# Moving the ring of streamed weight sums from 64 to 128 modulo 256 bytes in each partition

## The chip, the cores and the metric

The kernel runs on one core of a Trainium2 chip. The metric is device time in microseconds (us) of one launch, lower being better. Times come from plain runs, and from one profiled execution whose trace has a span from its first to its last instruction.

## The reference, cut to what matters

```python
# attention: batch 4, 8 heads, 768 rows, head dimension 64, fp32
k_sum = k.reshape(B, H, nb, 32, D).max(axis=3)          # one summary key per 32 rows
v_sum = v.reshape(B, H, nb, 32, D).mean(axis=3)
scores_l = where(|i - j| < 16, scale * q @ k.T, -1e9)   # local window
scores_s = scale * q @ k_sum.T + log(32)                # 24 summaries
a = softmax(concat([scores_l, scores_s]))
x = (a @ concat([v, v_sum]))  as 3072 rows of 512
# feed-forward: 512 -> 2048 -> 512
r = maximum(x @ w_in, 0)
out = (s * r * r + b) @ w_out
```

## The kernel before, in words

The 3072 rows are worked through in 12 chunks of 256, c = 0 to 11. For each chunk the kernel computes the windowed attention, then the first product (`hidden`, L512, into the PSUM tile `ph`), then square, scale and offset, then the second product into the output. The second product is `project` (L557) in chunks 0 to 3 and `project_seven` (L677) in chunks 4 to 11. The work of one chunk's attention is laid between the previous chunks' products. One long string, `ORDER`, written out by hand, sets in which order all of it is issued; no scheduler reorders it. In `ORDER`, `H7.12` is `hidden(7, 12)`, `p7.6.2` is `project_seven(7, 6, 2)` and `j7.6.0` is `load_combo(7, 6, 0)`.

All large products split each fp32 factor into an upper part and a remainder of the type fp32r, and add three products (remainder times upper, upper times remainder, upper times upper). In `hidden`, weights `wl` and `wh` are loaded into TensorE as the stationary operand (LDWEIGHTS, 128 columns), and the attention result `xh` or `xl`, 256 columns, is streamed through as the moving operand.

`project_seven` takes the feed-forward width in 8 pieces q of two 128-row blocks. It is a two by two block product with seven instead of eight multiplications. So it has seven products of three matmuls, 21 matmuls for each q and 64 such groups of 21 in all (8 chunks, 8 pieces). Here the activations `gs` are the stationary operand and 256 columns of weights the moving one. For the products 0, 1, 3 and 5 the moving operand is a piece of the resident weights `wh` or `wl`. For the products 2, 4 and 6 it is a sum of weight blocks, which is computed once, kept in HBM as `combos`, and streamed back for every chunk into the ring. So in a group the matmuls stand as six with resident weights, three with the ring, three resident, three ring, three resident, three ring.

The ring is one tile, `arena.tile([P, RING])`, of 3136 floats in each partition. Six slices of 512 floats lie in it: for q even or odd, three parts n, each with 256 floats of upper and 256 of remainder. `load_combo` (L617) fills one slice by one DMA of 256 KB, issued from SyncE's queue: 2048 bytes to each of 128 partitions. It waits until the matmuls that read the slice two pieces earlier are done. In the last chunk the last two pieces (q = 6 and 7) don't use the ring but tiles named `late`, since their loads are issued ahead.

What matters for an address is where the program, as built, puts each tile in a partition. These places are the same before and after the change, save for the slices within the ring.

| operand | role | start in the partition, modulo 256 bytes | modulo 512 |
|---|---|---|---|
| `wh`, `wl` | stationary in L512, moving in L677 | 0 | 256 |
| `xh`, `xl` | moving in L512 | 192 | 448 |
| `gs` | stationary in L677 | 192 | 192 |
| ring slices | moving in L677 | 64 | 320 |
| `late` for q = 6 and for q = 7, n = 2 | moving in L677 | 64 | 320 |
| `late` for q = 7, n = 0 and 1 | moving in L677 | 32 | 32 |

The ring's tile itself starts at byte 135424, which is 0 modulo 256. The same bytes serve earlier as `spare`, work space that starts at the tile's beginning and isn't touched by the change.

Of the kernel before, what the change touches and what calls it, by code (L numbers as in the profile page):

```python
# [45 lines left out]
def windowed_attention_then_relu2_ffn(ctx, tc, qk, vwin, kt, vt, kq, vrow, wp, out):  # L46
# [553 lines left out]
    def ring_part(c, q, n):  # L600
        if "ring" not in held:
            held["ring"] = arena.tile([P, RING], F32R, name="ring", tag="ring")
        if c == NC - 1 and q > 5:
            if q == 7 and n < 2:
                if "late" not in held:
                    held["late"] = p3.tile([P, 2 * UNIT], F32R, name="late", tag="qk", bufs=2)
                return held["late"][:, 512 * n : 512 * (n + 1)]
            if ("late", q, n) not in held:
                held["late", q, n] = p3.tile([P, 512], F32R, name="late", tag="vw", bufs=4)
            return held["late", q, n]  # L610
        k = 16 + 512 * (3 * (q % 2) + n)
        return held["ring"][:, k : k + 512]

    STREAMED = (T2, T3, T4)
# [1 line left out]
    def load_combo(c, q, n):  # L616
        nc.sync.dma_start(ring_part(c, q, n).bitcast(F32), combos[q, :, STREAMED[n]].rearrange("p h d -> p (h d)"))  # L617
# [44 lines left out]
    def project_seven(c, q, n):  # L662
        gh, gl = halves[c, q]
        if (q, n) == (0, 0):
            acc["m"] = ps_v.tile([P, DM], F32, name="acc", tag="pav")
            acc["x"], acc["y"] = (ps_po.tile([P, DM], F32, name="acc", tag="po") for _ in range(2))
            acc["z"] = ps_t.tile([P, DM], F32, name="acc", tag="pt")
        a, part, odd, lo, bank, side = PRODUCTS[n]
        if part is None:
            wh, wl = (w[2 * q + odd][:, lo : lo + 256] for w in (w_h, w_l))  # L670
        else:
            both = ring_part(c, q, part)
            wh, wl = both[:, :256], both[:, 256:]
        k = slice(a * P, (a + 1) * P)
        to = acc[bank][:, 256 * side : 256 * (side + 1)]
        for m, (g, w) in enumerate(((gl, wh), (gh, wl), (gh, wh))):
            nc.tensor.matmul(  # L677
                to, g[:, k], w, start=(q == 0 and side == 0 and m == 0),
                stop=(q == NF // 2 - 1 and m == 2 and side == (bank != "m")),
            )  # L680
# [301 lines left out]
```

## Time and profile before

| | |
|---|---|
| median of three plain runs | 595.0 us (593.6, 595.0 and 1473.68) |
| the profiled execution's own time | 593.89 us |
| its span | 592.2 us |
| TensorE matmuls busy | 579.7 us, 98% of the span |
| TensorE weight loads busy | 551.2 us, 93% |
| VectorE, ScalarE, GpSimd busy | 429.7, 352.3, 313.6 us |
| loads into the ring | 186 DMAs of 256 KB |

In the profile, PE is TensorE's matmuls and PEld its weight loads; a row names line, engine, operation, output and inputs, shapes and a count. The durations given for one matmul include its way through the array, and successive matmuls overlap. So the pace of TensorE is read from the distance between the starts of successive rows, not from the durations. Time 0 of all rows is the start of the span.

### The profile page before, as it was taken

The page shows a single profiled execution, that of the slowest core. Times are in us where ns is not written, and L with a number is a line of the kernel's source. Part 1 is how long each engine was busy: PE and PEld are TensorE (multiplying, and loading weights), DVE is VectorE, ACT ScalarE, POOL GpSimd, SP SyncE. Part 2 cuts the span into 40 slices and gives each one's busy share as a digit, 9 for nine tenths or more (in the row PEclk, how much of TensorE's full clock was granted, in tenths as well). Part 3 has the DMA queues.
Part 4 walks back from the last instruction along what each step waited for, and adds up shares of the span by engine and source line. Part 5 has one row for each costly group of instructions (what it writes and reads, how often), then busy time and mean ns, then how long its engine had stood idle before and what let it go on. Part 6 is the DMA issues. An engine that isn't in the chain of part 4 may idle for free.

```text
span 592.2 us, 15380 instructions
## 1 busy us (share of the span) xinstructions
PE 579.7 (98%) x5816; PEld 551.2 (93%) x5816; DVE 429.7 (73%) x1025; ACT 352.3 (59%) x808; POOL 313.6 (53%) x499
## 2 busy tenths in 40 slices
PE   7999999999999999999999999999999999999996
PEld 6788888989899899999999999999999999999996
DVE  6999977889697497699689699696687687322323
ACT  5999899367587683744654654653563564423432
POOL 4330012353665485357856756766747655636653
PEclk9999999999999999999999999999999999999999
DMA  8999964267656977876867977667566665574540
GB/s 337 401 390 412 360 232 157 85 214 228 210 168 216 306 251 244 285 228 226 265 235 239 274 222 230 230 200 232 189 196 223 203 198 182 178 223 153 170 143 35
DMA packets 69881, 135.73 MB, mean 229 GB/s; under 512 B 7792, under 2 KB 18032, under 8 KB 69808
## 3 DMA queue, kind: packets, MB, share of 16 engines
q1 hardware_dynamic: 69808, 134.77, 68.7%
q8 instruction: 45, 0.74, 0.5%
q14 instruction: 28, 0.23, 0.1%
HBM read 115.72 MB, written 18.87 MB: 227 GB/s over the span
## 4 chain that ended last, share of the span: by engine, by line
PE 80%; DMA 9%; DVE 5%; ACT 3%; issue 1%; POOL 1%; SPq 0%; DVEq 0%; POOLq 0%; ACTq 0%
PE ph L512 38%; PE acc L677 25%; PE po L557 10%; DMA wraw<-in_wp_dram 6%; PE pav L444 3%; PE ps L312 3%; DMA parked<-wf 1%; ACT pr L354 1%; DVE wf L135 1%; DMA kq<-in_kq_dram 1%; DVE spare L335 1%; DVE wf L134 1%; POOL g L583 0%; ACT wraw L125 0%; DVE wl L150 0%
## 5 line engine op out<-in xcount | busy, mean ns | idle before, releaser
L598 DVE TENSOR_TENSOR gs<-g,gs 128x896 fp32r<-128x896 f32 x64 | 71.5, 1118 | 82.7 <-ACT gs L594 82.0
L570 ACT ACTIVATE g<-ph 128x512 f32<-128x512 f32 x64 | 38.3, 598 | 153.1 <-PE ph L512 148.2
L393 DVE STREAM_TRANSPOSE pT<-qk 32x256 f32<-32x256 f32 x288 | 125.6, 436 | 4.8
L677 PE MATMUL acc<-wh,gs 128*128 128x256 f32 x512 | 121.4, 280 | 0.2 <-DVE gs L598 0.2
L512 PE MATMUL ph<-xh,wl 128*128 128x256 f32 x760 | 118.9, 278 | 1.2 <-ACT r L520 1.0
L512 PE MATMUL ph<-xh,wh 128*128 128x256 f32 x760 | 117.4, 276 | 0.0
L512 PE MATMUL ph<-xl,wh 128*128 128x256 f32 x760 | 117.4, 276 | 0.0
L578 POOL TENSOR_SCALAR g<-g,sb_col 128x512 f32<-128x512 f32 x64 | 54.8, 856 | 114.0 <-ACT g L574 105.7
L512 PEld LDWEIGHTS ph<-xh,wl 128*128 128x128 f32 x760 | 103.0, 188 | 5.4 <-ACT r L520 1.2
L512 PEld LDWEIGHTS ph<-xl,wh 128*128 128x128 f32 x760 | 100.7, 188 | 0.0
L512 PEld LDWEIGHTS ph<-xh,wh 128*128 128x128 f32 x760 | 100.5, 188 | 0.0
L677 PE MATMUL acc<-ring,gs 128*128 128x256 f32 x558 | 95.9, 280 | 0.0
L677 PEld LDWEIGHTS acc<-wh,gs 128*128 128x128 f32 x512 | 91.3, 188 | 1.5 <-issue 0.8
L677 PEld LDWEIGHTS acc<-ring,gs 128*128 128x128 f32 x558 | 78.8, 188 | 0.0
L557 PE MATMUL po<-wh,gs 128*128 128x512 f32 x224 | 76.7, 394 | 0.5 <-DVE gs L544 0.5
L583 POOL TENSOR_TENSOR g<-g 128x256 f32<-128x256 f32 x64 | 72.0, 1125 | 4.8
L677 PE MATMUL acc<-wl,gs 128*128 128x256 f32 x256 | 71.3, 278 | 0.0
L594 ACT CAST gs<-g 128x896 fp32r<-128x896 f32 x64 | 59.9, 935 | 16.4 <-PE acc L677 12.1
L354 ACT ACTIVATE qk<-qk,mn 128x120 f32<-128x120 f32 x144 | 55.0, 384 | 6.8 <-DVE mn L335 5.5
L274 POOL COPY vw<-vsum 24x256 f32<-24x256 f32 x88 | 44.0, 536 | 20.4 <-DMA vw<-in_vwin_dram 10.6
L557 PEld LDWEIGHTS po<-wh,gs 128*128 128x128 f32 x224 | 42.1, 188 | 9.1 <-DVE gs L544 0.7
L557 PE MATMUL po<-wl,gs 128*128 128x512 f32 x128 | 50.2, 392 | 0.0
(133 smaller groups left out, 901.2 us busy)
## 6 DMA issues: line engine op xcount, KB each, us to landing
ring<-combos SPq DMA_DIRECT2D x186, 256.0 KB
wraw<-in_wp_dram SPq DMA_DIRECT2D x32, 512.0 KB
qk<-in_qk_dram SPq DMA_DIRECT2D x44, 369.0 KB
vw<-in_vwin_dram SPq DMA_DIRECT2D x48, 256.0 KB
combos<-spare SPq DMA_DIRECT2D x16, 512.0 KB
out_dram<-o SPq DMA_DIRECT2D x24, 256.0 KB
kraw<-in_kt_dram SPq DMA_DIRECT2D x12, 384.0 KB
spare<-parked SPq DMA_DIRECT2D x8, 512.0 KB
```

Source lines behind the costliest of these rows:

```text
L274: nc.gpsimd.tensor_copy(vw_t[c, p][WIN:KR, e], vsum[bi][WIN : WIN + NB, 2 * p + e, :].unsqueeze(1).to_broadcast([NB, NSUB, D]),)
L312: nc.tensor.matmul(o, qi, kw[r, i, :], start=True, stop=True)
L354: nc.scalar.activation(pr, pr, AF.Exp, bias=mn_of[c, p][:, n : n + 1], scale=-1.0, accum_out=sums_of(c, p)[:, n : n + 1])
L393: nc.vector.transpose(to[BLOCK * k : BLOCK * (k + 1), :, rows], src)
L512: nc.tensor.matmul(ph, w[:, kc * P : (kc + 1) * P], x[:, kc], start=(n == 0), stop=(n == len(terms) - 1))
L557: nc.tensor.matmul(po[c, t], a[:, t * P : (t + 1) * P], w[:, 512:], start=(f == 0 and n == 0), stop=(f == NF - 1 and n == len(terms) - 1),)
L570: nc.scalar.activation(gg[c, q][:, : 2 * T], ph_of.pop((c, q)), AF.Relu)
L578: nc.gpsimd.tensor_scalar(g, g, s_col, b_col, ALU.mult, ALU.add)
L583: nc.gpsimd.tensor_tensor(g[:, 4:6], g[:, 0:1].to_broadcast([P, 2, P]), g[:, 1:3], ALU.subtract)
L594: nc.scalar.copy(halves[c, q][0], gg[c, q][:, P:])
L598: nc.vector.tensor_tensor(gl, gg.pop((c, q))[:, P:], gh.bitcast(F32), ALU.subtract)
L677: nc.tensor.matmul(to, g[:, k], w, start=(q == 0 and side == 0 and m == 0), stop=(q == NF // 2 - 1 and m == 2 and side == (bank != "m")),)
```

## The change

```diff
         if c == NC - 1 and q > 5:
...
             return held["late", q, n]
-        k = 16 + 512 * (3 * (q % 2) + n)
+        k = 32 + 512 * (3 * (q % 2) + n)
         return held["ring"][:, k : k + 512]
```

Every slice of the ring starts 32 floats past the tile's beginning instead of 16, and so at 128 modulo 256 bytes (384 modulo 512) instead of 64 (320). The tile has room for that: the last slice ends at float 3104 of 3136. The change touches the addresses of 186 DMAs (where they write) and of 558 matmuls (from where they read the moving operand). The instructions, their order on each engine, their waits and the places of all other tiles stay as they are, the `late` tiles' too.

## The prediction

> **What bounds the kernel now.** First the page's busy shares and its chain, then the costliest groups.
>
> ```profile
> PE 579.7 (98%) x5816; PEld 551.2 (93%) x5816; DVE 429.7 (73%) x1025; ACT 352.3 (59%) x808; POOL 313.6 (53%) x499
> PE 80%; DMA 9%; DVE 5%; ACT 3%; issue 1%; POOL 1%; SPq 0%; DVEq 0%; POOLq 0%; ACTq 0%
> L677 PE MATMUL acc<-wh,gs 128*128 128x256 f32 x512 | 121.4, 280 | 0.2 <-DVE gs L598 0.2
> L512 PE MATMUL ph<-xh,wl 128*128 128x256 f32 x760 | 118.9, 278 | 1.2 <-ACT r L520 1.0
> L677 PE MATMUL acc<-ring,gs 128*128 128x256 f32 x558 | 95.9, 280 | 0.0
> ```
>
> TensorE is the bound, and 80% of the chain that ended last. The last column matters most here: before the 558 matmuls that read the ring TensorE idled 0.0 us, so no load into the ring was ever late enough to hold it. The change can therefore act in two ways: on the pace at which TensorE reads the ring, directly on the bound; or on the loads, if they grew by more than their slack.
>
> The clock takes no part, since the stretches of time show it fully granted where the ring is used (the first of these rows stands for the others up to 592 us, all at 1.00).
>
> ```profile
> 240.00:300.00 60.00, 60.00 (x709) 59.42 (x705) 49.06 (x133) 35.53 (x101) 38.11 (x67) 1.00 0.80 254
> ```
>
> **The pace of TensorE.** This is a piece of its timeline: one group of 21 (403.17 to 405.62), the 24 matmuls of the first product behind it, and the next group's first row. The columns are the start in us, the length of the merged row, and what it is.
>
> ```profile
> 403.17 0.28 PE L677 MATMUL acc<-wh,gs 128*128 128x256 f32 x1
> ...
> 403.86 0.51 PE L677 MATMUL acc<-ring,gs 128*128 128x256 f32 x3
> 404.20 0.28 PE L677 MATMUL acc<-wh,gs 128*128 128x256 f32 x1
> 404.32 0.28 PE L677 MATMUL acc<-wl,gs 128*128 128x256 f32 x1
> ...
> 404.56 0.52 PE L677 MATMUL acc<-ring,gs 128*128 128x256 f32 x3
> 404.91 0.28 PE L677 MATMUL acc<-wh,gs 128*128 128x256 f32 x1
> ...
> 405.26 0.52 PE L677 MATMUL acc<-ring,gs 128*128 128x256 f32 x3
> 405.62 0.62 PE L512 MATMUL ph<-xh,wl 128*128 128x256 f32 x4
> 406.08 0.62 PE L512 MATMUL ph<-xl,wh 128*128 128x256 f32 x4
> ...
> 408.35 0.28 PE L677 MATMUL acc<-wh,gs 128*128 128x256 f32 x1
> ```
>
> From start to start, every matmul here having 256 columns:
> - first product, settled: 406.08 to 408.35, 20 matmuls in 2.27 us, 113.5 ns each;
> - the six resident ones before the first ring product: 403.17 to 403.86, 0.69 us, 115 ns each;
> - from the end of the first ring product to the end of the group: 404.20 to 405.62, 12 matmuls in 1.42 us, 118.3 ns each.
>
> So TensorE has two paces, about 113.5 and 118 ns, and in this group it changes from the fast to the slow one at the first ring product. Within the slow stretch the ring costs no more than the resident weights: three ring matmuls take 0.35 us (404.56 to 404.91), three resident ones 0.36 us (404.20 to 404.56). The first four matmuls of the next product still take 0.46 us (405.62 to 406.08, 115 ns each), and then the fast pace is back.
>
> The slow pace does not need the ring, though. A chunk's first two groups come right after the attention's small matmuls, and are slow from their second matmul on, before any ring product:
>
> ```profile
> 425.32 0.39 PE L677 MATMUL acc<-wh,gs 128*128 128x256 f32 x1
> 425.55 0.28 PE L677 MATMUL acc<-wl,gs 128*128 128x256 f32 x1
> ...
> 426.14 0.52 PE L677 MATMUL acc<-ring,gs 128*128 128x256 f32 x3
> ...
> 430.38 0.62 PE L512 MATMUL ph<-xh,wl 128*128 128x256 f32 x4
> ```
>
> Five resident matmuls from 425.55 to 426.14 take 118 ns each, and all 41 from 425.55 to 430.38 take 4.83 us, 117.8 ns each. [...]
>
> **The change part by part.** Nothing is added, removed or reordered; two terms remain.
>
> *Reads, 558 matmuls.* At 64 modulo 256 they cost 280 ns of duration, as the resident ones at 0 do (rows above), and at the slow pace the same 117 to 118 ns. The matmuls of the first product read their moving operand at 192 and run at 113.5 ns. The last chunk's tiles named late, partly at 32, are close:
>
> ```profile
> L677 PE MATMUL acc<-late,gs x18: 278/282/287, 582.5 to 587.1; 128*128 128x256 f32 x18
> ```
>
> So none of 0, 32, 64 and 192 shows a price of its own beyond 2 ns of duration, and 128 was not seen. I take 0 for it. The bounds: the best case is that at 128 the first ring product no longer brings the slow pace. From 403.86 to 406.08, 19 matmuls take 2.22 us, and at 113.5 ns they would take 2.16 us: 0.063 us for a group. The chain shows how many groups are like that one up to 574 us, where TensorE stops being the bound (its last row of the first product is at 571.41): 44 single groups, of which the first and last rows stand here, and the pair at 556.14, whose 4.92 us shows that it too starts fast.
>
> ```profile
> 251.46 2.44 PE acc L677 x21
> ...
> 425.39 5.15 PE acc L677 x42
> ...
> 556.14 4.92 PE acc L677 x42
> ...
> 568.96 2.44 PE acc L677 x21
> 571.41 2.74 PE ph L512 x24
> ```
>
> 45 x 0.063 = 2.8 us. If ring products at 128 even led back to the fast pace, as the first product does, the seven pairs like that at 425.39 would gain too, each at most 4.83 - 41 x 0.1135 = 0.18 us, together 1.2 us, and the second group of the pair at 556.14 some 0.1 us. So the reads save at most 4.1 us. The worst case is priced under the rivals.
>
> *Writes, 186 loads.* Each moves 256 KB whichever way it lies. What hides them is the time between issue and use:
>
> ```profile
> 399.23 7.29 SPq L617 DMA_DIRECT2D ring<-combos  x6
> ...
> 409.03 0.51 PE L677 MATMUL acc<-ring,gs 128*128 128x256 f32 x3
> ```
>
> The first of the six at 399.23 is the part j7.7.0, which was waiting for the ring product of piece 5 to free the slice; it is first read at 409.03, 9.8 us later. The core moved 254 GB/s in the busiest stretch quoted, at which 256 KB are 1.0 us of transfer. A load could take several times as long before TensorE saw it. Cost: 0. Behind the waiting SyncE instruction stand other loads, but what it waits for is TensorE, whose order stays.
>
> [...]
>
> Sum: 593.89 us for the profiled execution, whose span is 592.2 us with 1.7 us around it, plus 0, makes **593.9 us**. The median of the plain runs, 595.0, lies 1.1 us higher and their lowest, 593.6, 0.3 us lower, which is the scatter I allow.
>
> **The rivals.**
>
> *The first ring product stops breaking the pace* (faster, within 2%). For it: the pace changes just where the first operand at 64 is read, and nothing else in the group is new there but a wait for a landed load and another slice of `gs`. The distance between moving and stationary operand modulo 512 is 192 in the first product, which restores the fast pace (448 - 256); it is 64 with resident weights (256 - 192), 128 with the ring, and would be 192 for the ring after the change. Against it: ring and resident matmuls run alike in the slow stretch, and that stretch arises without the ring too. It gives 593.9 - 2.8 = 591.1 us, or 589.8 us if the slow pairs are healed as well.
>
> [...]
>
> *Ring matmuls clash with weight loads at 128* (slower). [...] The largest step that the rows show is 404.20 to 404.32, 0.12 us against the settled 0.1135, so 6.5 ns: 558 x 6.5 ns = 3.6 us, and 597.5 us. It decides as soon as a ring matmul costs more than the 118 ns of the slow pace. For it: 128 was never seen, and TensorE has no idle time to hide it. Against it: four other places without such a cost. To be slower by 2% (11.9 us), it would have to be 21 ns for each ring matmul, three times the largest step seen.
>
> *The loads become late*: only if one took over 9.8 us in place of some 1 to 3. No row speaks for it, and I leave it 1 in 100. That the change fails to do what it says can be left out, as the ring's tile starts at 0 modulo 256.
>
> **How the numbers follow.** No change: 0.44, 593.9 us, with the scatter 593.5 to 595. The pace kept or restored: 0.33, 589.8 to 591.1 us. A clash in the ring's reads: 0.21, up to 597.5 us, and 0.01 of it beyond 2%. Late loads: 0.01. The remaining 0.01 is for a gain beyond 2%, for which no mechanism is in sight: all ring matmuls together are far from 21 ns above the fast pace. The range from 589.5 to 597.5 us takes in the bounds of both unknowns. About 2%, 11.9 us, is what a measurement of this kernel can tell from no change; every priced case lies within that, so faster 0.01, same 0.97, slower 0.02.
>
> **What the profile after would show.** If I am right, the timeline again shows 113.5 ns in the first product, 115 ns up to the first ring product and 117 to 118 ns behind it, groups of 2.44 us and pairs of 5.15 us in the chain. If the first rival holds, groups of 21 take about 2.39 us and ring matmuls start every 0.113 us. If the second holds, three ring matmuls take more than 0.36 us while resident ones stay. Idle time before the ring's matmuls, now 0.0, would mean late loads. What would make me wrong beyond the range is a cost of 128 in TensorE's reads that no other operand here has.

## The result, and the profile after

The changed kernel takes 600.84 us (median of 6 runs, 600.05 to 601.47) against 594.35 us for the kernel before (median of its runs on the same chip). The ratio is 1.0111, 95% interval 1.0088 to 1.0135: slower by about 6.5 us. One of the six launches before, of 1473.68 us, is far above all the others: the median hardly feels it, and the ratio leaves it out. The forecast was 593.9 us, and 600.84 lies above the range's upper end of 597.5.

The page of the kernel after, with the rows that answer to those of before:

```profile
PE 586.5 (98%) x5816; PEld 558.1 (93%) x5816; DVE 429.6 (72%) x1025; ACT 352.2 (59%) x808; POOL 311.7 (52%) x499
L677 PE MATMUL acc<-wh,gs 128*128 128x256 f32 x512 | 122.9, 283 | 0.2 <-DVE gs L598 0.2
L512 PE MATMUL ph<-xh,wl 128*128 128x256 f32 x760 | 120.8, 281 | 0.3 <-DVE wl L150 0.2
L512 PE MATMUL ph<-xl,wh 128*128 128x256 f32 x760 | 119.6, 280 | 0.0
L512 PE MATMUL ph<-xh,wh 128*128 128x256 f32 x760 | 119.6, 280 | 0.0
L677 PE MATMUL acc<-ring,gs 128*128 128x256 f32 x558 | 95.5, 280 | 0.0
```

TensorE is busy 6.8 us longer (586.5 after 579.7), which is the whole loss. But the 558 matmuls whose addresses changed are no dearer: 95.5 us in place of 95.9, and still no idle time before them. The first product, whose addresses nobody touched, is what costs more: 120.8 us in place of 118.9 in the first of its three groups, and 119.6 in place of 117.4 in each of the others.

The busy times by stretches place it. First before, then after; the columns are the stretch, its length, the busy time and count of PE, PEld, VectorE, ScalarE and GpSimd, then the granted clock (1.00 is full speed), the busy share of the DMA engines and GB/s. Each stretch ends shortly after the last first product.

```profile
244.00:575.00 331.00, 331.00 (x3389) 329.04 (x3388) 226.57 (x531) 166.11 (x388) 206.42 (x315) 1.00 0.68 215
```

```profile
244.00:581.00 337.00, 337.00 (x3379) 335.01 (x3378) 226.28 (x527) 165.35 (x387) 203.12 (x312) 1.00 0.66 210
```

From 244 us on, where the ring is in use, TensorE needs 6 us more for nearly the same number of matmuls, without a gap and at the full clock in both.

The chain of waits shows in which pieces. Two rows of the first product from the kernel before, whose groups of 21 took 2.44 us:

```profile
405.78 2.73 PE ph L512 x24
...
416.13 5.45 PE ph L512 x48
```

And after:

```profile
400.96 2.47 PE acc L677 x21
403.43 2.83 PE ph L512 x24
406.26 2.47 PE acc L677 x21
...
419.33 5.65 PE ph L512 x48
```

A group of 21 takes 2.47 us where it took 2.44. The 24 matmuls of the first product between two groups take 2.83 us where they took 2.73, and the double ones at a chunk's end 5.65 where they took 5.45. From the first group to the last first product either chain has 44 single groups, 45 single first products and 7 double ones: 44 x 0.03 + 45 x 0.10 + 7 x 0.20 = 7.2 us by these rounded rows, against 6.6 us that the span grew (592.2 to 598.8). Of the difference 0.4 us is found ahead of the first group, which starts at 243.07 us after and at 243.51 before; the rest is rounding.

A piece of the timeline of the kernel after, one group and the first product behind it:

```profile
406.09 0.28 PE L677 MATMUL acc<-wh,gs 128*128 128x256 f32 x1
...
406.80 0.52 PE L677 MATMUL acc<-ring,gs 128*128 128x256 f32 x3
407.15 0.28 PE L677 MATMUL acc<-wh,gs 128*128 128x256 f32 x1
...
408.21 0.51 PE L677 MATMUL acc<-ring,gs 128*128 128x256 f32 x3
408.57 0.63 PE L512 MATMUL ph<-xh,wl 128*128 128x256 f32 x4
409.04 0.63 PE L512 MATMUL ph<-xl,wh 128*128 128x256 f32 x4
...
411.39 0.28 PE L677 MATMUL acc<-wh,gs 128*128 128x256 f32 x1
```

Everything now runs at the slow pace. The six resident matmuls from 406.09 to 406.80 take 118 ns each (115 before), the three of the ring 0.35 us, and the first product from 408.57 to 411.39 takes 2.82 us, 117.5 ns each. Before, it was back at the fast pace of 113.5 ns after four matmuls. Now it never gets there, and hands the slow pace on to the next group.

### The profile page after: what moved, and what is told of

The parts are those of the page before. It is cut to its first block, busy times and chain, and to the rows that moved or that the text cites. A ratio compares the mean times of both kernels' runs of the same rounds, so it can differ in the third digit from the quotient of the medians.

```text
span 598.8 us, 15380 instructions
## 1 busy us (share of the span) xinstructions
PE 586.5 (98%) x5816; PEld 558.1 (93%) x5816; DVE 429.6 (72%) x1025; ACT 352.2 (59%) x808; POOL 311.7 (52%) x499
## 4 chain that ended last, share of the span: by engine, by line
PE 81%; ACT 10%; DVE 3%; DMA 2%; issue 1%; POOL 1%; SPq 0%; DVEq 0%; POOLq 0%; ACTq 0%
PE ph L512 38%; PE acc L677 25%; PE po L557 10%; PE pav L444 4%; PE ps L312 3%; ACT wraw L125 2%; ACT wraw L126 2%; DMA wraw<-in_wp_dram 2%; ACT spare L354 1%; DVE wf L135 1%; ACT wh L230 1%; ACT r L531 1%; ACT r L520 1%; DMA kq<-in_kq_dram 1%; ACT r L526 1%
## 5 line engine op out<-in xcount | busy, mean ns | idle before, releaser
L677 PE MATMUL acc<-wh,gs 128*128 128x256 f32 x512 | 122.9, 283 | 0.2 <-DVE gs L598 0.2
L512 PE MATMUL ph<-xh,wl 128*128 128x256 f32 x760 | 120.8, 281 | 0.3 <-DVE wl L150 0.2
L512 PE MATMUL ph<-xl,wh 128*128 128x256 f32 x760 | 119.6, 280 | 0.0
L512 PE MATMUL ph<-xh,wh 128*128 128x256 f32 x760 | 119.6, 280 | 0.0
L512 PEld LDWEIGHTS ph<-xh,wh 128*128 128x128 f32 x760 | 102.6, 189 | 0.0
L512 PEld LDWEIGHTS ph<-xl,wh 128*128 128x128 f32 x760 | 102.4, 189 | 0.0
L677 PE MATMUL acc<-ring,gs 128*128 128x256 f32 x558 | 95.5, 280 | 0.0
L677 PEld LDWEIGHTS acc<-wh,gs 128*128 128x128 f32 x512 | 91.7, 188 | 1.4 <-issue 0.8
L677 PEld LDWEIGHTS acc<-ring,gs 128*128 128x128 f32 x558 | 79.0, 188 | 0.0
L677 PE MATMUL acc<-wl,gs 128*128 128x256 f32 x256 | 71.6, 280 | 0.0
L274 POOL COPY vw<-vsum 24x256 f32<-24x256 f32 x88 | 42.2, 517 | 17.1 <-issue 8.4
```

Source lines behind the costliest of these rows:

```text
L274: nc.gpsimd.tensor_copy(vw_t[c, p][WIN:KR, e], vsum[bi][WIN : WIN + NB, 2 * p + e, :].unsqueeze(1).to_broadcast([NB, NSUB, D]),)
L512: nc.tensor.matmul(ph, w[:, kc * P : (kc + 1) * P], x[:, kc], start=(n == 0), stop=(n == len(terms) - 1))
L677: nc.tensor.matmul(to, g[:, k], w, start=(q == 0 and side == 0 and m == 0), stop=(q == NF // 2 - 1 and m == 2 and side == (bank != "m")),)
```

## The experiments

Two questions were asked: is it the reading or the writing of the ring, and what decides at which pace the first product runs? The theory that grew from the rows above: TensorE has two paces for a stream of weight loads and 256-column matmuls, about 113.5 and 117.5 ns; which of them a first product gets is decided as it is entered, by what is read directly ahead of it. The rivals: a share of the loss for each ring matmul; a cost of writing at 128; a cost that grows with the offset.

Ratios are to runs of the kernel before made beside each experiment (medians 593.51 to 594.35 us), with 95% intervals.

In the three kernels that write and read at different places, each read of a slice takes 16 floats of its neighbour. What they compute is therefore not the reference's output; the work and its order are the same, and only their time is used.

### Writing at 128, reading from 64, first try

```diff
-RING = 3136
+RING = 3264
...
-    def ring_part(c, q, n):
+    def ring_part(c, q, n, at=16):
...
+            for lo in (16, 1552, 1680, 3216):
+                nc.gpsimd.memset(held["ring"][:, lo : lo + 16].bitcast(F32), 0.0)
...
-        k = 16 + 512 * (3 * (q % 2) + n)
+        k = at + 1664 * (q % 2) + 512 * n
...
-        nc.sync.dma_start(ring_part(c, q, n).bitcast(F32), ...
+        nc.sync.dma_start(ring_part(c, q, n, 32).bitcast(F32), ...
```

> The loads write at 128 modulo 256, the matmuls read from 64 (so each reads 16 floats that belong to its neighbour slice; the ring has a gap between the slices of even and odd pieces, is 512 bytes longer, and its edges are cleared once). Reading theory (the place from which the matmuls read decides): about 594.4 us, ratio to the kernel before 1.00, groups of 21 matmuls 2.44 us and 24 matmuls of the first product 2.73 us. Writing theory (the loads' place in the partition decides): about 600.8 us, ratio 1.011, 2.47 and 2.83 us.

Measured: 1089.12 us, ratio 1.8327 (1.8271 to 1.8383). It answers neither theory, since the edit made a wait of its own. The 16 floats that a read shares with the slice below it are written by a load that stands ahead of that read in the hand-written order, so TensorE waited for that load. Besides, the granted clock was only 0.80 in the mean of the run, against 1.00 in the kernel before. From the view of waits (who waited for what, us in all, times, the longest):

```profile
PE acc L679 <- DMA ring<-combos: 328.1, 115, 5.1
```

The two lines added for the ring's edges make L679 here what is L677 in the others.

### Writing at 64, reading from 128

The same edit as in the first try, but with the two places exchanged:

```diff
-    def ring_part(c, q, n):
+    def ring_part(c, q, n, at=32):
...
+        nc.sync.dma_start(ring_part(c, q, n, 16).bitcast(F32), ...
```

> The converse: the loads write at 64, the matmuls read from 128. Reading theory: about 600.8 us, ratio 1.011, groups of 21 matmuls 2.47 us and the first product 2.83 us. Writing theory: about 594.4 us, ratio 1.00, 2.44 and 2.73 us.

Measured: 601.21 us, ratio 1.0121 (1.0098 to 1.0144). Its chain:

```profile
392.16 2.83 PE ph L512 x24
394.99 2.47 PE acc L679 x21
```

The whole loss is there though the loads write where they did before.

### Writing at 128, reading from 64, without the new wait

The first try once more, with the parts of a piece in falling order in the ring (the diff is against the first try):

```diff
-        k = at + 1664 * (q % 2) + 512 * n
+        k = at + 1664 * (q % 2) + 512 * (2 - n)
```

> Loads write at 128, matmuls read from 64, with the parts of a piece in falling order in the ring, so that the 16 floats that a read shares with its neighbour slice bring no new wait (each read takes 16 floats of the neighbour's data). Reading theory: about 593.7 us, ratio 1.00, 2.44 us for a group of 21 and 2.73 us for the first product's 24. Writing theory: about 601 us, ratio 1.012, 2.47 and 2.83 us.

Measured: 593.14 us, ratio 0.9992 (0.9982 to 1.0002).

```profile
389.92 2.73 PE ph L512 x24
392.65 2.44 PE acc L679 x21
```

No wait for the ring stands in its chain from 239 to 575 us, where 43 of 44 groups take 2.44 us. So the place from which TensorE reads decides, and where the loads write costs nothing that can be measured. That holds for the loads themselves too, and not only because they are hidden: in the packet records of the trace from 250 to 560 us, the 2048-byte packets, most of them ring loads, took 84 ns in the median in the kernel after, which writes at 128 too, and in the kernel before alike.

### Which of a group's three ring products matters

Only the third part's slices at 128 (last128), and only those at 64 (last64):

```diff
-        k = 16 + 512 * (3 * (q % 2) + n)
+        k = 512 * (2 * (q % 2) + n) + 16 if n < 2 else 2080 + 512 * (q % 2)
```

```diff
-        k = 16 + 512 * (3 * (q % 2) + n)
+        k = 512 * (2 * (q % 2) + n) + 1056 if n < 2 else 16 + 512 * (q % 2)
```

> Only the slices of the third part (n = 2), which the last product of each group reads directly ahead of the first product, lie at 128; the other two parts stay at 64. Exit theory (what is read directly ahead of the first product decides whether that product finds back to the fast pace): about 600 us, ratio 1.010, first product 2.83 us for 24. Count theory (each matmul that reads at 128 costs its own share, wherever it stands): a third of the loss, about 596.5 us, ratio 1.0037.

> The converse: the third part at 64, the first two parts at 128. Exit theory: about 594.5 us, ratio 1.000, first product 2.73 us for 24. Count theory: two thirds of the loss, about 598.7 us, ratio 1.0074.

Measured: last128 600.97 us, ratio 1.0121 (1.0100 to 1.0142); last64 593.83 us, ratio 1.0003 (0.9991 to 1.0016). Their chains, last128 first:

```profile
401.30 2.47 PE acc L677 x21
403.78 2.83 PE ph L512 x24
```

```profile
402.53 2.44 PE acc L677 x21
404.97 2.73 PE ph L512 x24
```

A third of the ring matmuls at 128 brings all of the loss, and the other two thirds bring none. A share for each ring matmul is excluded. Here the product that stands directly ahead of the first product is the one that counts.

### Resident weights last

The changed kernel, with `p7.5.6` ahead of `p7.5.5` in `ORDER`, and so on for the pieces 1 to 6 of each chunk:

```diff
-p7.5.4 us7.6 tb9.0.0.3 af7.7 p7.5.5 j7.7.1 p7.5.6
+p7.5.4 us7.6 tb9.0.0.3 af7.7 p7.5.6 j7.7.1 p7.5.5
```

> The changed kernel (all slices at 128), with the last two products of a group in the other order for the pieces 1 to 6, so that resident weights and not the ring are read directly ahead of the first product; the same matmuls, loads and addresses. Exit theory in its narrow form (a ring read at 128 directly ahead of the first product is what leaves it slow): the first product is back at 2.73 us for 24 behind those groups and the time at about 594 us, ratio 1.00. If what stands last is only one of several ways into the slow pace: still 2.83 us and about 601 us, ratio 1.012.

Measured: 595.08 us, ratio 1.0025 (1.0013 to 1.0037). The chain shows why it isn't quite 1.00:

```profile
410.22 2.74 PE ph L512 x24
412.96 2.44 PE acc L677 x21
415.40 5.65 PE ph L512 x48
```

Behind the swapped groups the first product is fast again, although all the ring lies at 128. Behind piece 7, where the order was kept, the double first product still takes 5.65 us. The seven of these before 575 us cost 7 x 0.20 = 1.4 us, about the 1.6 us by which the run was slower (593.51 us for the kernel before beside it). The swap also puts two ring products one behind the other; whether that matters, beside what stands last, was not separated.

### Is it a place or a distance

The kernel before with 64 bytes more ahead of all large tiles, so that the ring lies at 128 as in the changed kernel, and the weights, `gs`, `xh` and `xl` have moved with it:

```diff
-    sb_col = const.tile([P, 2], F32, name="sb_col")
+    sb_col = const.tile([P, 18], F32, name="sb_col")[:, :2]
```

> The kernel before, with 64 bytes more ahead of all large tiles, so that the ring, the weights, gs, xh and xl all lie 64 bytes further: the ring at 128 modulo 256 as in the changed kernel, but at the same distance from the others as before. Distance theory (the distance between the moving operand and the weights being loaded decides): 593.7 us, ratio 1.00, 2.44 and 2.73 us. Place theory (a place of the ring itself, modulo 256, decides): about 601 us, ratio 1.012, 2.47 and 2.83 us, or another time altogether.

Measured: 594.15 us, ratio 1.0006 (0.9995 to 1.0017).

```profile
405.51 2.73 PE ph L512 x24
408.24 2.44 PE acc L677 x21
```

A ring at 128 is harmless if everything else lies 64 further too. So it is the place of the operands to each other that counts. Which of the distances is the one that acts (ring to `gs`, or ring to the first product's weights, or several) was not taken apart.

### The other offsets

One number changes in each: k = 0, 8, 24, 40, 48, 56 or 64 plus 512 * (3 * (q % 2) + n), for the offsets 0 to 256 bytes.

> The ring's slices at 0 modulo 256 (256 modulo 512), the place of the resident weights, no other edit. Place theory (only the place of the moving operand matters): a ring product is then like a resident one, nothing breaks the fast pace within a group, groups of 21 take 2.39 us, the first product 2.72 us, and the time is about 590.8 us, ratio 0.995. Ring theory (the first ring product breaks the pace wherever it lies, by its wait for a load or its other slice of gs): 593.7 us if the exit is like that at 64, 601 us if it is like that at 128.

> Slices at 32 modulo 256, so at a distance of 96 from gs (64 keeps either pace, 128 breaks the fast one but leaves the first product fast). Two-state theory: the first product's 24 take 2.72 to 2.74 or 2.83 us and nothing between, the time lies between 590 and 601 us according to their shares. Gradual theory (the cost grows with the distance): between the runs at 0 and at 64 in each group alike, first products all of one length, 594 to 595.7 us.

> Slices at 96, distance 160, half way between the kernel before and the changed one. Two-state theory: first products of 2.72 to 2.74 or 2.83 us only; about 594, about 601 or a share of both. Gradual theory: all first products about 2.78 us and about 597.5 us.

> Slices at 160, distance 224. Two-state theory: as above, with ring matmuls dearer than 118 ns as at 192 (distance 0 modulo 256) possible, so 594 to 602 us. Gradual theory: first products all alike, between the runs at 128 and 192, about 600 us.

> The ring's slices at 192 modulo 256 (448 modulo 512), the place of xh and xl. Two-state theory (the first product runs either at 113.4 or at 117.8 ns for a matmul, and what is read ahead of it decides which): 2.73 or 2.83 us for its 24, so about 594 or about 601 us and nothing between. Gradual theory (the time grows with the distance from 64): beyond the value at 128, about 607 us, and 2.9 us or more for the 24.

> Slices at 224, distance 32, between 192 (599 us, dear ring matmuls) and 256 (595.5 us). Two-state theory: first products of 2.72 to 2.74 or 2.83 us only, 592 to 602 us. Gradual theory: all alike, about 597 us.

> All slices at 0 modulo 256 again, but at 0 modulo 512, where the run with slices at 0 had 256. If the pattern repeats every 256 bytes: the same alternation of first products of 2.73 and 2.83 us and about 595.7 us, ratio 1.004. If it repeats only every 512 bytes or more: another sequence, with a time that differs, still out of 2.72 to 2.74 and 2.83 us pieces.

| offset in bytes | us | ratio, interval | groups of 21, us | first products, us |
|---|---|---|---|---|
| 0 | 595.70 | 1.0041, 1.0026 to 1.0056 | 2.38 and 2.47 in turn | 2.73 and 2.83 in turn |
| 32 | 595.35 | 1.0024, 1.0013 to 1.0036 | 2.46 | 2.74 |
| 64 (before) | 594.35 | 1 | 2.44 | 2.73 |
| 96 | 600.49 | 1.0117, 1.0102 to 1.0132 | 2.47 | 2.83 |
| 128 (changed) | 600.84 | 1.0111, 1.0088 to 1.0135 | 2.47 | 2.83 |
| 160 | 593.05 | 0.9986, 0.9973 to 0.9999 | 2.42 | 2.73 |
| 192 | 598.97 | 1.0095, 1.0080 to 1.0110 | mostly 2.48 and 2.52 in turn | mostly 2.72 and 2.83 in turn |
| 224 | 601.00 | 1.0132, 1.0107 to 1.0157 | 2.47 | 2.83 |
| 256 | 595.46 | 1.0028, 1.0016 to 1.0039 | 2.38 and 2.47 in turn | 2.73 and 2.83 in turn |

The table gives the single pieces of each chain up to 575 us. At every offset a first product takes either 2.72 to 2.75 or 2.83 us and nothing between, while the times go up and down along the table. A cost that grows with the offset is excluded. At 256 the pattern of 0 comes back; so it repeats with 256 bytes, for this pair at least.

The most telling chain is that of offset 0:

```profile
393.10 2.47 PE acc L677 x21
395.57 2.73 PE ph L512 x24
398.30 2.38 PE acc L677 x21
400.69 2.83 PE ph L512 x24
403.51 2.47 PE acc L677 x21
```

Here nothing breaks the pace within a group: one that follows a fast first product stays fast (2.38 us, 113.4 ns each), one that follows a slow one stays slow. But a group that ends fast throws the next first product into the slow pace, and one that ends slow is followed by a fast one, so the two alternate. The addresses modulo 256 and the instructions are the same each time, and only the history differs. That even and odd pieces use different slices of the ring isn't the cause: piece 2 is fast in chunk 9 (2.38 us at 479.23) and slow in chunk 10 (2.47 us at 523.20).

### Two mixtures

The first two ring products of a group at 0, which leaves the pace alone, and the last at 64 (mix0_64) or at 160 (mix0_160):

```diff
-        k = 16 + 512 * (3 * (q % 2) + n)
+        k = 512 * (2 * (q % 2) + n) if n < 2 else 2064 + 512 * (q % 2)
```

```diff
-        k = 16 + 512 * (3 * (q % 2) + n)
+        k = 512 * (2 * (q % 2) + n) if n < 2 else 2088 + 512 * (q % 2)
```

> The first two ring products of a group read at 0 modulo 256, the last at 64. Two-state theory, put together from the runs so far (at 0 a ring product leaves the fast pace alone; a group that leaves in the slow pace by a read at 64 is followed by a fast first product): groups of 21 about 2.39 us, the first product 2.73 us, about 591.3 us, ratio 0.996. If instead a group that stays fast nearly to its end always throws the next first product into the slow pace, as with all slices at 0: every second first product or all of them 2.83 us, 595 to 597 us, ratio 1.003 to 1.006.

> The first two ring products of a group read at 0, which left the fast pace alone, the last at 160, behind which every first product was fast. If the pace ahead of the last ring product and the distance of that product decide what follows (two-state theory), it joins both: groups of 21 about 2.39 us, all first products 2.73 us, about 592 us, ratio 0.997. If what follows depends on more of the history than that: some first products of 2.83 us, as when the last was put at 64, and 594 to 597 us.

Measured: mix0_64 595.80 us, ratio 1.0037 (1.0022 to 1.0051); mix0_160 591.38 us, ratio 0.9958 (0.9942 to 0.9973). In the chain of mix0_64 one chunk alternates and another stays slow throughout:

```profile
397.29 2.72 PE ph L512 x24
400.01 2.39 PE acc L677 x21
402.40 2.83 PE ph L512 x24
405.23 2.48 PE acc L677 x21
407.70 2.72 PE ph L512 x24
...
532.64 2.83 PE ph L512 x24
535.47 2.48 PE acc L677 x21
537.95 2.83 PE ph L512 x24
```

That was a miss of mine: from "64 is followed by a fast first product" I had put it together, but in the kernel before the last ring product at 64 is reached at the slow pace, and here, behind a fast first product, at the fast one. That explains the alternating chunk and not the other: the groups at 405.23 and at 535.47 both take 2.48 us, slow from end to end, and read at the same places modulo 256, yet the first product behind them takes 2.72 us in one case and 2.83 in the other. So the pace and the places do not settle it alone; what else takes part is not shown. At 160 the rows had shown a fast first product behind a last ring product that was reached fast. So that mixture was foreseen:

```profile
401.98 2.39 PE acc L677 x21
404.37 2.73 PE ph L512 x24
```

It beats both kernels, by 2.5 us against the one before (593.88 us beside it). Of its first products up to 575 us one takes 2.83 us, 44 take 2.73 to 2.75 us.

## Why the prediction was wrong, step by step

*That TensorE bounds the kernel, without slack, and that there are two paces:* right. Busy time grew by 6.8 us and the span by 6.6 us, and the rows show 113.5 and 117.5 ns. What inside TensorE makes the two paces no run shows.

*Writes, 186 loads, cost 0:* right. Writing at 128 gave the ratio 0.9992 (0.9982 to 1.0002), and no wait for the ring stands in that run's chain. No price shows in the packets either, whose median is 84 ns written at 64 and at 128.

*Reads, 558 matmuls, 0:* this is the step that failed, in its value and even more in its bounds. I priced the reads by the matmuls that make them, and they did stay at 280 ns. The price fell on the first product behind them, 2.83 in place of 2.73 us. I had read its 2.73 us as a property of the product, which "restores the fast pace", when it was a property of how it is entered. That a slow stretch lasts, as the 41 matmuls at 117.8 ns each showed, I applied to groups of 21 alone. Had I let it reach over the first product, the worst bound would have been 24 matmuls at 117.5 in place of 113.5 ns, 0.10 us for each of some 60 first products, so about 6 us more. That is most of what came; the rest is 0.03 us for each of 44 groups, which are now entered at the slow pace. The row that should have warned me stood in the prediction: the first four matmuls of the first product still took 115 ns each, so it starts within the slow pace and has to find out of it.

*The first rival, the pace kept or restored:* wrong in its sign at 128. Its idea, that the distance between the operands counts, was right (all64, ratio 1.0006). But the distance of 192 that the ring then has to `gs` did not restore the pace (groups of 2.47 us, first products of 2.83 us).

*The second rival, a clash at each ring matmul:* the right sign, the wrong place. Its point of decision, a ring matmul above 118 ns, was not reached (0.35 us for three together), and yet the kernel lost 6.5 us. With its place limited to the ring's own matmuls, its 3.6 us could not reach 6.5 us. That reads of the ring clash with weight loads was my guess; no row shows it.

*No case beyond 2%:* right, at 1.1%.

## What to carry to other kernels

Where an engine is busy without a gap, read its pace from start to start, and ask of each stretch whether its pace belongs to it or was handed to it by what ran ahead; then bound a change by all that stands behind it on the engine, not by the instructions that it edits. The moving and the stationary operands of such a stream should be looked at by their distance modulo 256 bytes (offsets 0 and 256 gave the same pattern here, at 595.70 and 595.46 us), and a few offsets should be tried on the chip, because the best of those tried (here 0, 0 and 160, for 0.4%) depends on what stands next to each other. Such a pattern can turn with a small edit elsewhere, as it did here with the swap of two products (first products of 2.74 in place of 2.83 us).

## What the runs showed of the hardware that was not expected

- This kernel's stream of fp32r weight loads of 128 columns with matmuls of 256 columns ran at two lasting paces, about 113.5 and 117.5 ns for a pair, at the same clock (1.00), the same instructions and the same addresses modulo 256 bytes. At offset 0 both alternate through one run (first products of 2.73 and 2.83 us).
- The place of the operands to each other bears on the changes between them: the first ring product at 64 breaks the fast pace (115 ns for a matmul ahead of it and 118.3 behind it, in the kernel before), at 0 it doesn't (groups of 2.38 us, 113.4 ns each), and all tiles together moved by 64 bytes change nothing (ratio 1.0006). It doesn't decide alone, as mix0_64 shows (2.72 and 2.83 us behind groups of 2.48 us).
- At 192, where the ring lies like `gs` modulo 256, about every second group takes 2.52 us, more than the 2.47 us of the slow pace.
- The place within 256 bytes to which 2048-byte rows of a load are written made no difference: 84 ns for a packet in the median and the ratio 0.9992, written at 128 in place of 64.
